# Attention backward in a fused block: query-major E by TensorE transposes and word copies instead of recomputed scores

## The chip, the cores and the metric

The kernel runs on 1 core of one Trainium2 chip. Time is device microseconds of one execution; three runs of the kernel before took 2842.46, 2846.36 and 2848.7 us, so the median is 2846.36 us.

## The reference

The program is forward and backward of a block `out = x + A(xn) * silu(B(xn))` with `xn = layernorm(x)`: A is multi-head attention, B is a layernorm and an MLP. It returns `out` and the gradients of seven inputs. S = 2048 tokens, D = 512, H = 32 heads of 16 numbers each, F = 1792, all in bf16. What concerns the change is attention and its backward:

```python
qkv = (x @ wqkv).reshape(B, S, 3, H, Dh).transpose(2, 0, 3, 1, 4)
q, k, v = qkv[0], qkv[1], qkv[2]
scores = jnp.einsum("bhqd,bhkd->bhqk", q, k) * (Dh ** -0.5)
p = _softmax(scores, axis=-1)
o = jnp.einsum("bhqk,bhkd->bhqd", p, v)
return o.transpose(0, 2, 1, 3).reshape(B, S, D) @ wo
...
_out, _vjp = jax.vjp(_f, A_x, A_wqkv, A_wo, B_w1, B_b1, B_w2, B_b2)
```

With E = exp(scores - bound) and G = E * (dO v^T), the outputs o and dq are sums over keys of E and G, and dk and dv are sums over queries of E and G. The first kind of sum wants E and G with keys on the partitions, the second with queries on the partitions.

## The kernel before

There are three phases: layernorms, projections and the MLP's forward (`phase_pre`), attention forward and backward together (`attention_core`), and the rest of the backward (`phase3`). The change lies in `attention_core` alone, whose instructions stand in the order in which its Python emits them, engine by engine (`tc.manual_schedule()`).

The 32 heads go as 16 pairs. A pair has 4 query chunks of 512 queries; a pair with a query chunk is a block (64 blocks), and a block has 16 steps, one for each key block `kb` of 128 keys. The two heads of a pair are `hj` 0 and 1. `KVT` and `QDT` hold a pair's operands with 32 rows for each of k (or q) of both heads and v (or dO) of both heads, so a matmul over them uses a quarter of the array's rows; the sums X and Z use a quarter of the columns each.

Step g does, for its key block:
- **s**, L649: scores, keys on partitions, both heads into one tile of two PSUM banks; ScalarE makes `et` from them (L677, 1024 wide). It is emitted one step ahead.
- **d**, L663: dO v^T, a bank for each head (`ps_d`, two banks); VectorE multiplies it with `et` into `gts` (L698, 512 wide, twice a step).
- **l, e, g**, L730, L733 and L745, of the step before: sums over keys into X (row sums of E, E with v and k, G with k). After 16 steps X is copied to `xs` (L751, VectorE).
- a query block of the block before, by `b_unit`: the sums over queries. They need E and G with queries on the partitions. For G, SyncE issues DMA transposes `gk<-gts` (L711), one every two steps. For E there are two ways: query blocks 1 and 3 of each key chunk come by DMA transposes `ek<-et` (L717; `dma_units`), the other two are computed again: **t**, L635, scores with queries on the partitions into the same two-bank pool as s (`ps_st`, two tiles), and a second exponential `e` (L685, 1024 wide). Then `Z<-e` or `Z<-ek` (L808) and `Z<-gk` (L814) add to Z, 64 partitions for one key chunk of 512 keys. After the four query blocks VectorE adds Z to `acc` (L819, L821).

```python
        emit_t(g)
        if not first:
            emit_le(g - 1)
        emit_exp_b(g)
        emit_s(g + 1)
        emit_d(g)
        emit_mult(g)
        emit_exp_a(g + 1)
        emit_dmat(g)
        if first:
            emit_le(g - 1)
        emit_g(g - 1)
        emit_z(g - lagb, 0)
        emit_z(g - lagb, 1)
```

One step after a block's last, `emit_finalize` transposes `xs` on TensorE (`XT`, L761, in one of d's banks), VectorE copies it (`xt`, L763) and computes three small tiles, and GpSimd makes the weights W1 and W2 that Z needs. The next pair's operands are loaded by `load_ops` in the second block of a pair: plain loads, copies into `KVPad` and `QDPad` on GpSimd, two DMA transposes `KVT` and `QDT` on SyncE (L595, L603).

Of the kernel before, what the change touches and what calls it, by code (L numbers as in the profile page):

```python
# [542 lines left out]
def attention_core(ctx, tc, NAT_s, NATQ_s, Oall, dQall, dKVT_out, ident_f32, npairs=16, nqc=4):  # L543
    nc = tc.nc
    dma_units = tuple((kc, qb) for kc in range(4) for qb in (1, 3))
    lagb = 3
    sb = lambda name, bufs: ctx.enter_context(tc.tile_pool(name=name, bufs=bufs))
    opnd = sb("opnd", 1)
    ps_st = ctx.enter_context(tc.tile_pool(name="ps_st", bufs=2, space=PSUM))
    ps_d = ctx.enter_context(tc.tile_pool(name="ps_d", bufs=2, space=PSUM))  # L550
# [3 lines left out]
    gtp = sb("gtp", 4)  # L554
    gbp = sb("gbp", 5)
    ekp = sb("ekp", 10)
    ep = sb("ep", lagb + 2)
    xsp = sb("xsp", 1)
    finp = sb("finp", 2)
# [12 lines left out]
    KVPad = opnd.tile([128, 16, 4, 32], bf16, name="KVPad")  # L572
    QDPad = opnd.tile([128, 16, 4, 32], bf16, name="QDPad")
    nc.gpsimd.memset(KVPad[:], 0.0)
    nc.gpsimd.memset(QDPad[:], 0.0)
# [4 lines left out]
    acc = opnd.tile([64, S], f32, name="acc")  # L580

    def load_ops(p):
        t = OP[p % 2]

        def plain():
            nc.sync.dma_start(out=t["NAT"][:].rearrange("q k j c -> q k (j c)"), in_=NAT_s[p])
            nc.sync.dma_start(out=t["NATQq"][:].rearrange("q k j c -> q k (j c)"), in_=NATQ_s[0][p])
            nc.sync.dma_start(out=t["NATQd"][:].rearrange("q k j c -> q k (j c)"), in_=NATQ_s[1][p])

        def ck():  # L590
            nc.gpsimd.tensor_copy(out=KVPad[:, :, 0:2, 0:17], in_=t["NAT"][:, :, :, 0:17])
            nc.gpsimd.tensor_copy(out=KVPad[:, :, 2:4, 0:16], in_=t["NAT"][:, :, :, 17:33])

        def tk():
            nc.sync.dma_start_transpose(out=t["KVT"][:].rearrange("r (m k) -> r m k", m=16),  # L595
                                        in_=KVPad[:].rearrange("q m j c -> q (m j c)"))

        def cq():
            nc.gpsimd.tensor_copy(out=QDPad[:, :, 0:2, 0:17], in_=t["NATQq"][:])
            nc.gpsimd.tensor_copy(out=QDPad[:, :, 2:4, 0:16], in_=t["NATQd"][:])  # L600

        def tq():
            nc.sync.dma_start_transpose(out=t["QDT"][:].rearrange("r (m k) -> r m k", m=16),  # L603
                                        in_=QDPad[:].rearrange("q m j c -> q (m j c)"))
        return [plain, ck, cq, tk, tq]
# [4 lines left out]
    st_s, st_t, st_d, st_et, st_e, st_gt = {}, {}, {}, {}, {}, {}  # L610
# [6 lines left out]
    def b_unit(g):  # L617
        j = g // 16 - 1
        return (j, (g % 16) // 4, g % 4) if 0 <= j < NB else None
# [4 lines left out]
    def emit_t(g):  # L624
        b = b_unit(g)
        if b is None or b[1:] in dma_units:
            return
        j, kc, qb = b
        op = op_of(j)
        q0 = (blocks[j][1] * 4 + qb) * 128  # L630
        t = ps_st.tile([128, 2, 512], f32, name="t", tag="st")
        st_t[g] = t
        for hj in range(2):
            r = 32 * hj
            nc.tensor.matmul(t[:, hj, :], lhsT=op["QDT"][r:r + 32, q0:q0 + 128], rhs=op["KVT"][r:r + 32, kc * 512:(kc + 1) * 512],  # L635
                             start=True, stop=True, tile_position=(r, 0))

    def emit_s(g):
        a = a_unit(g)
        if a is None:  # L640
            return
        j, kb = a
        op = op_of(j)
        qc = blocks[j][1]
        s = ps_st.tile([128, 2, 512], f32, name="s", tag="st")
        st_s[g] = s
        for hj in range(2):
            r = 32 * hj
            nc.tensor.matmul(s[:, hj, :], lhsT=op["KVT"][r:r + 32, kb * 128:(kb + 1) * 128], rhs=op["QDT"][r:r + 32, qc * 512:(qc + 1) * 512],  # L649
                             start=True, stop=True, tile_position=(r, 0))  # L650

    def emit_d(g):
# [6 lines left out]
        ds = []  # L659
        for hj in range(2):  # L660
            r = 64 + 32 * hj
            d = ps_d.tile([128, 512], f32, name="d", tag="d")
            nc.tensor.matmul(d[:], lhsT=op["KVT"][r:r + 32, kb * 128:(kb + 1) * 128], rhs=op["QDT"][r:r + 32, qc * 512:(qc + 1) * 512],  # L663
                             start=True, stop=True, tile_position=(r, 0))
            ds.append(d)
        st_d[g] = ds

    def emit_exp_a(g):
        a = a_unit(g)
        if a is None:  # L670
            return
        kb = a[1]
        if kb % 4 == 0:
            cur["et"] = etp.tile([128, 4, 4, 2, 128], bf16, name="et")
        et = cur["et"]
        st_et[g] = et
        nc.scalar.activation(out=et[:, :, kb % 4, :, :].rearrange("k b h q -> k h b q"),  # L677
                             in_=st_s.pop(g)[:].rearrange("k h (b q) -> k h b q", b=4), func=ACT.Exp)

    def emit_exp_b(g):  # L680
        if g not in st_t:
            return
        e = ep.tile([128, 2, 512], bf16, name="e")
        st_e[g] = e
        nc.scalar.activation(out=e[:], in_=st_t.pop(g)[:], func=ACT.Exp)  # L685

    def emit_mult(g):
# [8 lines left out]
        ds = st_d.pop(g)  # L696
        for hj in range(2):
            nc.vector.tensor_tensor(out=gts[:, kb % 2, hj, :].rearrange("k (b q) -> k b q", b=4), in0=ds[hj][:].rearrange("k (b q) -> k b q", b=4),  # L698
                                    in1=st_et[g][:, :, kb % 4, hj, :], op=ALU.mult)

    def emit_dmat(g):
# [10 lines left out]
        if kb % 4 == 3:  # L712
            for qb in range(4):
                if (kc, qb) in dma_units:
                    ek = ekp.tile([128, 8, 128], bf16, name="ek")
                    blk[j]["Ek"][(kc, qb)] = ek
                    nc.sync.dma_start_transpose(out=ek[:], in_=st_et[g][:, qb].rearrange("k a h q -> k (a h q)"))  # L717

    def emit_le(g):
# [4 lines left out]
        if kb == 0:  # L724
# [4 lines left out]
        for hj in range(2):  # L729
            nc.tensor.matmul(X[64 + 32 * hj:96 + 32 * hj, :], lhsT=Lc[:], rhs=et[:, :, kb % 4, hj, :],  # L730
                             start=(kb == 0), stop=False, skip_group_check=True, tile_position=(0, 64 + 32 * hj))
        for hj in range(2):
            nc.tensor.matmul(X[32 * hj:32 * hj + 32, :], lhsT=NATt[:, kb, hj, 1:33], rhs=et[:, :, kb % 4, hj, :],  # L733
                             start=(kb == 0), stop=(kb == 15), tile_position=(0, 32 * hj))

    def emit_g(g):
        a = a_unit(g)
        if a is None:
            return
        j, kb = a  # L740
        X = blk[j]["X"]
        NATt = op_of(j)["NAT"]
        gts = st_gt[g]
        for hj in range(2):
            nc.tensor.matmul(X[64 + 32 * hj:64 + 32 * hj + 17, :], lhsT=NATt[:, kb, hj, 0:17], rhs=gts[:, kb % 2, hj, :],  # L745
                             start=False, stop=(kb == 15), skip_group_check=True, tile_position=(0, 64 + 32 * hj))
        st_et.pop(g)
        st_gt.pop(g)
        if kb == 15:
            xs = xsp.tile([128, 512], f32, name="xs")  # L750
            nc.vector.tensor_copy(out=xs[:], in_=X[:])  # L751
            blk[j]["xs"] = xs

    def emit_finalize(j):
        p, qc = blocks[j]
        NQq = op_of(j)["NATQq"]
        NQd = op_of(j)["NATQd"]
        xs = blk[j].pop("xs")
        XT = ps_d.tile([128, 4, 128], f32, name="XT", tag="d")
        for qb in range(4):  # L760
            nc.tensor.transpose(XT[:, qb, :], xs[:, qb * 128:(qb + 1) * 128], ident_f32[:])  # L761
        xt = finp.tile([128, 4, 128], f32, name="xt")
# [14 lines left out]
        nc.vector.scalar_tensor_tensor(out=ndr[:], in0=dl[:], scalar=-1.0, in1=rL[:], op0=ALU.mult, op1=ALU.mult)  # L777
        nc.gpsimd.tensor_tensor(out=W1[:, :, :, 0:16], in0=ndo, in1=bc(rL[:]), op=ALU.mult)  # L778
        nc.gpsimd.tensor_tensor(out=W2[:, :, :, 16:32], in0=nqs, in1=bc(rL[:]), op=ALU.mult)
# [13 lines left out]
    def emit_z(g, part):  # L793
        b = b_unit(g)
        if b is None:
            return
        j, kc, qb = b
        p, qc = blocks[j]
        if part == 0:
            if qb == 0:  # L800
                cur["Z"] = ps_z.tile([64, 512], f32, name="Z", tag="z")
            Z = cur["Z"]
            if (kc, qb) in dma_units:
                ev = blk[j]["Ek"].pop((kc, qb))[:].rearrange("q (a h) k -> q h a k", h=2)
            else:
                ev = st_e.pop(g)[:].rearrange("q h (a k) -> q h a k", a=4)
            for hj in range(2):
                nc.tensor.matmul(Z[32 * hj:32 * hj + 32, :], lhsT=blk[j]["W1"][:, qb, hj, :], rhs=ev[:, hj],  # L808
                                 start=(qb == 0), stop=False, tile_position=(0, 32 * hj))
            return  # L810
        Z = cur["Z"]
# [155 lines left out]
```

## Time and profile before

| | us |
|---|---|
| median of three runs | 2846.36 |
| profiled execution, span | 2837.7 |
| PE busy | 2383.5 (84%) |
| VectorE (DVE) busy | 2013.4 (71%) |
| ScalarE (ACT) busy | 1739.4 (61%) |
| GpSimd (POOL) busy | 620.1 (22%) |
| `gts` multiplies L698, 2048 of them | 681 ns each |
| `et` exponentials L677, 1024 of them | 1024 ns each |
| `e` exponentials L685, 512 of them | 1023 ns each |
| DMA, mean | 192 GB/s, under 512 B 1,754,785 of 1,831,694 packets |

The profiled execution's own time is its span of 2837.7 us, from its first to its last instruction; the runs' times lie some 9 us above it. Busy times are of the whole program and overlap; the duration of a matmul holds its way through the array, so the distance between starts tells more than the duration. `x2` in a timeline row stands for two instructions of one kind in a row, and brackets hold the idle time before it and what ended it.

### The profile page before, as it was taken

The page shows a single profiled execution, that of the slowest core. Times are in us where ns is not written, and L with a number is a line of the kernel's source. Part 1 is how long each engine was busy: PE and PEld are TensorE (multiplying, and loading weights), DVE is VectorE, ACT ScalarE, POOL GpSimd, SP SyncE. Part 2 cuts the span into 40 slices and gives each one's busy share as a digit, 9 for nine tenths or more (in the row PEclk, how much of TensorE's full clock was granted, in tenths as well). Part 3 has the DMA queues.
Part 4 walks back from the last instruction along what each step waited for, and adds up shares of the span by engine and source line. Part 5 has one row for each costly group of instructions (what it writes and reads, how often), then busy time and mean ns, then how long its engine had stood idle before and what let it go on. Part 6 is the DMA issues. An engine that isn't in the chain of part 4 may idle for free. (4 is left out here: it accounts for less than half of the span.)

```text
span 2837.7 us, 49038 instructions
## 1 busy us (share of the span) xinstructions
PE 2383.5 (84%) x18885; PEld 779.8 (27%) x18944; DVE 2013.4 (71%) x3382; ACT 1739.4 (61%) x1973; POOL 620.1 (22%) x1023
## 2 busy tenths in 40 slices
PE   3786998989989998998989999899999857665967
PEld 2332222222222222222222222222222333332443
DVE  5764887878778787887878778788778638880044
ACT  3442777777777777777777777777777535440020
POOL 0434111101011110111101111110111328870024
PEclk8898899999999999999999999999999978887989
DMA  5434999999999999999999999999999853326331
GB/s 178 110 131 121 213 224 225 219 221 226 220 225 225 221 218 222 229 218 227 220 224 219 231 219 221 224 224 226 217 225 225 214 168 98 103 82 162 110 131 41
DMA packets 1831694, 543.46 MB, mean 192 GB/s; under 512 B 1754785, under 2 KB 1815586, under 8 KB 1831458
## 3 DMA queue, kind: packets, MB, share of 16 engines
q1 hardware_dynamic: 1758066, 486.70, 84.1%
q10 hardware_dynamic: 73392, 53.62, 6.1%
q8 instruction: 148, 2.42, 0.4%
q14 instruction: 88, 0.72, 0.1%
HBM read 65.41 MB, written 55.32 MB: 43 GB/s over the span
## 5 line engine op out<-in xcount | busy, mean ns | idle before, releaser
L698 DVE TENSOR_TENSOR gts<-d,et 128x512 bf16<-128x512 f32 x2048 | 1301.5, 681 | 379.4 <-issue 229.6
L677 ACT ACTIVATE et<-s 128x1024 bf16<-128x1024 f32 x1024 | 1000.5, 1024 | 29.8 <-PE d L663 11.5
L685 ACT ACTIVATE e<-t 128x1024 bf16<-128x1024 f32 x512 | 523.7, 1023 | 457.3 <-PE t L635 453.9
L663 PE MATMUL d<-QDT,KVT 32*128 32x512 bf16 x2048 | 598.1, 383 | 150.2 <-DVE gts L698 148.5
L649 PE MATMUL s<-QDT,KVT 32*128 32x512 bf16 x2048 | 402.8, 390 | 18.2 <-DMA QDT<-QDPad 13.2
L730 PE MATMUL X<-et,Lc 128*32 128x512 bf16 x2048 | 404.3, 391 | 14.3 <-DVE xs L751 14.3
L733 PE MATMUL X<-et,NAT 128*32 128x512 bf16 x2048 | 404.7, 392 | 0.0
L745 PE MATMUL X<-gts,NAT 128*17 128x512 bf16 x2048 | 402.4, 389 | 0.0
L814 PE MATMUL Z<-gk,W 128*32 128x512 bf16 x2048 | 401.0, 385 | 0.0
L778 POOL TENSOR_TENSOR W<-NATQd,rL 128x128 bf16<-128x128 bf16 x64 | 25.7, 402 | 1365.7 <-DVE rL L773 1365.7
L745 PEld LDWEIGHTS <-NAT 128*17 128x17 bf16 x2048 | 92.5, 87 | 491.5 <-issue 491.5
L808 PE MATMUL Z<-e,W 128*32 128x512 bf16 x1024 | 202.5, 389 | 4.7 <-DVE acc L821 2.3
L808 PE MATMUL Z<-ek,W 128*32 128x512 bf16 x1024 | 204.4, 395 | 0.0
L635 PE MATMUL t<-KVT,QDT 32*128 32x512 bf16 x1024 | 201.5, 390 | 0.0
L649 PEld LDWEIGHTS <-KVT 32*128 32x128 bf16 x2048 | 97.5, 91 | 361.7 <-issue 361.5
L663 PEld LDWEIGHTS <-KVT 32*128 32x128 bf16 x2048 | 138.7, 91 | 108.7 <-issue 80.4
L730 PEld LDWEIGHTS <-Lc 128*32 128x32 bf16 x2048 | 103.9, 93 | 181.6 <-issue 181.6
L821 DVE TENSOR_TENSOR acc<-Z,acc 64x512 f32<-64x512 f32 x192 | 129.1, 672 | 13.7 <-PE Z L814 13.7
L808 PEld LDWEIGHTS <-W 128*32 128x32 bf16 x2048 | 121.2, 93 | 57.4 <-issue 51.6
L733 PEld LDWEIGHTS <-NAT 128*32 128x32 bf16 x2048 | 101.3, 96 | 52.7 <-issue 3.5
L814 PEld LDWEIGHTS <-W 128*32 128x32 bf16 x2048 | 104.1, 96 | 8.2 <-issue 0.6
L635 PEld LDWEIGHTS <-QDT 32*128 32x128 bf16 x1024 | 48.3, 91 | 205.1 <-issue 205.1
(200 smaller groups left out, 2583.7 us busy)
## 6 DMA issues: line engine op xcount, KB each, us to landing
gk<-gts SPq DMA_TRANSPOSE x512, 4.1
ek<-et SPq DMA_TRANSPOSE x512, 3.1
HG_s<-hg SPq DMA_DIRECT2D x16, 448.0 KB, 3.1
DH_s<-dh ACTq DMA_DIRECT2D x16, 448.0 KB, 2.5
NAT<-NAT_s SPq DMA_DIRECT2D x16, 264.0 KB, 3.1
GB_s<-gB ACTq DMA_DIRECT2D x16, 256.0 KB, 2.0
dKVT_s<-ob SPq DMA_DIRECT2D x16, 256.0 KB, 3.4
dhc<-DH_s ACTq DMA_DIRECT2D x2, 2048.0 KB, 13.9
```

What stands on the lines that cost most here:

```text
L635: nc.tensor.matmul(t[:, hj, :], lhsT=op["QDT"][r:r + 32, q0:q0 + 128], rhs=op["KVT"][r:r + 32, kc * 512:(kc + 1) * 512], start=True, stop= ...
L649: nc.tensor.matmul(s[:, hj, :], lhsT=op["KVT"][r:r + 32, kb * 128:(kb + 1) * 128], rhs=op["QDT"][r:r + 32, qc * 512:(qc + 1) * 512], start ...
L663: nc.tensor.matmul(d[:], lhsT=op["KVT"][r:r + 32, kb * 128:(kb + 1) * 128], rhs=op["QDT"][r:r + 32, qc * 512:(qc + 1) * 512], start=True, ...
L677: nc.scalar.activation(out=et[:, :, kb % 4, :, :].rearrange("k b h q -> k h b q"), in_=st_s.pop(g)[:].rearrange("k h (b q) -> k h b q", b= ...
L685: nc.scalar.activation(out=e[:], in_=st_t.pop(g)[:], func=ACT.Exp)
L698: nc.vector.tensor_tensor(out=gts[:, kb % 2, hj, :].rearrange("k (b q) -> k b q", b=4), in0=ds[hj][:].rearrange("k (b q) -> k b q", b=4), ...
L730: nc.tensor.matmul(X[64 + 32 * hj:96 + 32 * hj, :], lhsT=Lc[:], rhs=et[:, :, kb % 4, hj, :], start=(kb == 0), stop=False, skip_group_check ...
L733: nc.tensor.matmul(X[32 * hj:32 * hj + 32, :], lhsT=NATt[:, kb, hj, 1:33], rhs=et[:, :, kb % 4, hj, :], start=(kb == 0), stop=(kb == 15), ...
L745: nc.tensor.matmul(X[64 + 32 * hj:64 + 32 * hj + 17, :], lhsT=NATt[:, kb, hj, 0:17], rhs=gts[:, kb % 2, hj, :], start=False, stop=(kb == 1 ...
L808: nc.tensor.matmul(Z[32 * hj:32 * hj + 32, :], lhsT=blk[j]["W1"][:, qb, hj, :], rhs=ev[:, hj], start=(qb == 0), stop=False, tile_position= ...
L814: nc.tensor.matmul(Z[32 * hj:32 * hj + 32, :], lhsT=blk[j]["W2"][:, qb, hj, :], rhs=gv[:, :, :, hj, qb, :], start=False, stop=(qb == 3), t ...
L821: nc.vector.tensor_tensor(out=av, in0=Z[0:64, :], in1=av, op=ALU.add)
```

## The change

The recomputed scores t and their exponential `e` are gone. E with queries on the partitions now comes from `et` alone: query block 3 of each key chunk by DMA transpose (a quarter), query blocks 0 to 2 by eight 128x128 transposes on TensorE into one PSUM bank (`tT`, new L694), which ScalarE copies to `ek` as 512 words of 32 bits, two bf16 numbers in each. A batch is emitted in three of four steps, four steps or more behind the exponential that made its `et`.

PSUM is dealt out anew: s has a bank for each head (`ps_st`, three tiles of one bank, shared with `tT`), and so ScalarE runs two 512-wide exponentials instead of one of 1024; `ps_d` has three banks instead of two. Two key chunks lie side by side in Z on 128 partitions, `acc` is `[128, 2, 512]`, and successive steps go to the lower and the upper half in turn (`ZORD`), so `acc` is added to twice a block instead of four times. `xs` moves from VectorE to ScalarE, `emit_finalize` is split in two and comes a step later, Z comes two steps later. `KVPad` and `QDPad` become one tile `Pad`, so the loads' order is copy, transpose, copy, transpose; a pair's result is stored with two DMAs instead of one. Buffers: `gtp` 4 to 3, `gbp` 5 to 7, `ekp` 10 to 19, `finp` 2 to 1, `ep` gone.

```diff
-    dma_units = tuple((kc, qb) for kc in range(4) for qb in (1, 3))
-    lagb = 3
-    ps_st = ctx.enter_context(tc.tile_pool(name="ps_st", bufs=2, space=PSUM))
-    ps_d = ctx.enter_context(tc.tile_pool(name="ps_d", bufs=2, space=PSUM))
+    ps_st = ctx.enter_context(tc.tile_pool(name="ps_st", bufs=3, space=PSUM))
+    ps_d = ctx.enter_context(tc.tile_pool(name="ps_d", bufs=3, space=PSUM))
...
-    gtp = sb("gtp", 4)
-    gbp = sb("gbp", 5)
-    ekp = sb("ekp", 10)
-    ep = sb("ep", lagb + 2)
+    gtp = sb("gtp", 3)
+    gbp = sb("gbp", 7)
+    ekp = sb("ekp", 19)
...
-    acc = opnd.tile([64, S], f32, name="acc")
+    acc = opnd.tile([128, 2, 512], f32, name="acc")
...
-        return [plain, ck, cq, tk, tq]
+        return [plain, ck, tk, cq, tq]
...
+    ZORD = [((i // 8) * 2 + i % 2, (i % 8) // 2) for i in range(16)]
...
+    def emit_s(g, hj):
...
+        s = ps_st.tile([128, 512], f32, name="s", tag="st")
+        nc.tensor.matmul(s[:], lhsT=op["KVT"][r:r + 32, kb * 128:(kb + 1) * 128], rhs=op["QDT"][r:r + 32, qc * 512:(qc + 1) * 512],
+                         start=True, stop=True, tile_position=(r, 0))
...
+        nc.scalar.activation(out=et[:, :, kb % 4, hj, :], in_=s[:].rearrange("k (b q) -> k b q", b=4), func=ACT.Exp)
...
         if kb % 4 == 3:
-            for qb in range(4):
-                if (kc, qb) in dma_units:
-                    ek = ekp.tile([128, 8, 128], bf16, name="ek")
-                    blk[j]["Ek"][(kc, qb)] = ek
-                    nc.sync.dma_start_transpose(out=ek[:], in_=st_et[g][:, qb].rearrange("k a h q -> k (a h q)"))
+            ek = ekp.tile([128, 8, 128], bf16, name="ek")
+            blk[j]["Ek"][(kc, 3)] = ek
+            nc.sync.dma_start_transpose(out=ek[:], in_=st_et[g][:, 3].rearrange("k a h q -> k (a h q)"))
+
+    def t_unit(g):
+        a = a_unit(g - 4)
+        if a is None or a[1] % 4 == 3:
+            return None
+        return a[0], a[1] // 4, a[1] % 4
+
+    def emit_T(g):
...
+        et = st_et[j * 16 + kc * 4 + 3]
+        t = ps_st.tile([128, 8, 128], bf16, name="tT", tag="st")
+        for b in range(8):
+            nc.tensor.transpose(t[:, b, :], et[:, qb, b // 2, b % 2, :], ident_bf[:])
+        st_T[g] = t
+
+    def emit_cT(g):
...
+        ek = ekp.tile([128, 8, 128], bf16, name="ek")
+        blk[j]["Ek"][(kc, qb)] = ek
+        nc.scalar.copy(out=ek[:].rearrange("q a k -> q (a k)").bitcast(f32),
+                       in_=st_T.pop(g)[:].rearrange("q a k -> q (a k)").bitcast(f32))
...
+            for hj in range(2):
+                r = 64 * par + 32 * hj
+                nc.tensor.matmul(Z[r:r + 32, :], lhsT=blk[j]["W2"][:, qb, hj, :], rhs=gv[:, :, :, hj, qb, :],
+                                 start=(qb == 0), stop=False, skip_group_check=True, tile_position=(0, r))
...
+    FIN_AT = 2
+    ZG, ZE = -5, -5
...
+        emit_z(g + ZG - 16, 1)
+        emit_z(g + ZE - 16, 0)
+        emit_acc(g + ZE - 16)
+        emit_s(g + 1, 0)
+        emit_XT(g)
+        emit_d(g, 0)
+        emit_d(g, 1)
+        emit_s(g + 1, 1)
+        emit_mult(g)
+        emit_fin(g)
+        emit_T(g)
+        emit_x(g - 1, "l")
+        emit_x(g - 1, "e")
+        emit_x(g - 1, "g")
+        emit_xs(g - 1)
+        emit_cT(g)
+        emit_dmat(g)
```

## The prediction

> **What bounds the kernel now.** I read the page's slices first, then the table of stretches for a quiet part of the attention, then the timeline of some of its steps, then the waits, and last the DMA issues of SyncE.
>
> ```profile
> PE   3786998989989998998989999899999857665967
> DVE  5764887878778787887878778788778638880044
> ACT  3442777777777777777777777777777535440020
> ...
> DMA  5434999999999999999999999999999853326331
> ```
> ```profile
> 800.00:1200.00 400.00, 363.49 (x3195) 98.12 (x3196) 315.77 (x537) 299.67 (x314) 57.88 (x150) 0.99 1.14 222
> ```
> The second fence is one row of the table of stretches: busy time of PE, PEld, DVE, ACT and POOL, then granted clock, DMA share and GB/s. Attention fills slices 5 to 31 and no engine but PE comes near full: in 400 us PE is busy 363, DVE 316, ACT 300. The first multiply `gts` starts at 283.47 us, the last step's at 2222.42; 1,023 steps between them make 1.895 us a step, 30.3 us for a block of 16 steps, 1,940 us for the 64 blocks. Everything else (some 900 us) the change doesn't touch. So the question is what one step costs.
>
> ```profile
> 999.95 0.39 PE L635 MATMUL t<-KVT,QDT 32*128 32x512 bf16 x2
> 1000.27 0.39 PE L730 MATMUL X<-et,Lc 128*32 128x512 bf16 x2
> 1000.28 0.39 PE L733 MATMUL X<-et,NAT 128*32 128x512 bf16 x2
> 1000.60 0.39 PE L649 MATMUL s<-QDT,KVT 32*128 32x512 bf16 x2
> 1000.61 0.39 PE L663 MATMUL d<-QDT,KVT 32*128 32x512 bf16 x2
> 1000.93 0.39 PE L745 MATMUL X<-gts,NAT 128*17 128x512 bf16 x2
> 1000.93 0.39 PE L808 MATMUL Z<-ek,W 128*32 128x512 bf16 x2
> 1001.16 0.38 PE L814 MATMUL Z<-gk,W 128*32 128x512 bf16 x2
> ...
> 1002.47 0.37 PE L663 MATMUL d<-QDT,KVT 32*128 32x512 bf16 x1 [0.23 <-DVE gts L698]
> ...
> 1003.31 0.39 PE L635 MATMUL t<-KVT,QDT 32*128 32x512 bf16 x2
> ```
> Starts count here, not durations. Matmuls on different quarters of the array start together: l (L730) and e (L733), s and d, g (L745) and `Z<-ek`. A pass that keeps its way of cutting the array (columns after columns) frees its quarters after 0.22 us (1000.93 to 1001.16); one followed by another cut, rows after columns or the reverse, after 0.32 (999.95 to 1000.27, 1000.28 to 1000.60). From the same timeline the passes of these two steps, without waits, are .32+.33+.32+.22 for t, le, sd, g with Z, then .22 and .31 for Z with the next l and for e, then .32+.22+.31: 2.57 us. They take 3.36 (999.95 to 1003.31), and the next two, with an `acc` on DVE, 3.65: 7.0 for four steps. The rest is waiting, and the row at 1002.47 says for what: d has two banks, and its next one is free only when `gts` has multiplied the one before. The waits put numbers to this and to a second limit:
>
> ```profile
> PE d L663 <- DVE gts L698: 148.5, 525, 3.7
> ...
> DVE gts L698 <- DMA gk<-gts: 58.3, 30, 4.5
> ```
> ```profile
> 1001.29 4.44 SPq L711 DMA_TRANSPOSE gk<-gts  x2
> 1005.83 2.65 SPq L717 DMA_TRANSPOSE ek<-et  x2
> 1008.58 3.58 SPq L711 DMA_TRANSPOSE gk<-gts  x2
> ```
> SyncE issues transposes without a pause, 7.29 us for the four of four steps. Matched in order, a `gk` transpose lands 9.0 us (median; 5.3 to 13.6 at the 5th and 95th percentile) after the multiply that fills its source has ended. When the loads of the next pair come between, it falls behind and `gts` finds no free buffer. Most blocks take 29.5 us from one `XT` to the next; these stalls make the mean 30.3.
>
> **The change part by part, for four steps (PE first).** Gone are t and ScalarE's exponential of it (two in four steps) and one of two `ek` transposes by DMA. Added are three batches T of eight 128x128 transposes. Their price comes from phase 3:
>
> ```profile
> 2426.13 0.61 PE L384 MATMUL h_tp<-ident_bf,h1T 128*128 128x128 bf16 x8
> ```
> ```profile
> 2433.46 1.54 ACT L422 COPY dh1T<-dh_tp 128x512 bf16<-128x512 bf16 x3
> ```
> Eight transposes span 0.61 with 0.22 for one alone, so they follow at 0.056; a batch and the cut after it take 7 x 0.056 + 0.15 = 0.54 (0.15: from the last f32 transpose `XT` to the next pass 0.205 passes where two of them are 0.109 apart, so 0.10 for the cut). From rows to the whole array the trace of before shows nothing; columns to the whole array took 0.31 (`Z` to `XT`) and 0.37 (`Z` to L52 at 2226.4), and I take 0.32, as for the other cuts.
>
> The Trainium skill, "TensorE: Matmul & The Clock Gate", section Back-to-back issue gap, speaks against this change: in a stream of weight loads and matmuls 128 columns wide it gives about 81 ns each; an estimate by it adds 8 x 0.025 us to each batch, 2.4 us to a block, which would turn the forecast below into 2,900 us, slower than before.
>
> The rest of the step on PE: s, d stay one pass (.32). l and e stay one pass, now followed by g without a new cut (.22). `Z<-gk` comes straight after g: in steps where Z is in the lower half of the partitions the two run together, as g and `Z<-ek` do at 1000.93, in the others it waits .22. `Z<-ek` follows on the same columns (.22) and a cut (.32) leads back to s. A step with T and the upper half is .32+.54+.22+.22+.22+.32 = 1.84; with the lower half 1.62; the step without T (every fourth, always lower half) .32+.22+0+.22+.32 = 1.08. Four steps: 1.84+1.62+1.84+1.08 = 6.38, against 5.14 before. So PE gets more to do; what may shrink is the waiting, 7.0 less 5.14.
>
> Does it? d now has three banks. d starts, DVE starts .51 later (1000.61 to 1001.12), multiplies follow at .60; the first d's bank is back .51+.69+.05 = 1.25 us after it and wanted one step later, the second's 1.85 and two steps: no wait. DVE has 8 x .60, half an `acc` of 128x512 (.30; two of 64 rows before, .60) and no `xs`: 5.1 in four steps, plus 1.35 a block for `xt` and the three small ones. ScalarE: two 1024-wide exponentials start .92 apart, three 512-wide copies take 1.54, so .48 each; 8 halves and 3 word copies are 5.3, as much as before (6 x .91 = 5.5), and `xs` adds .48 a block. The 32-bit copy reads and writes f32: L260, f32 to f32 of that size, has a mean of 595 ns, L422 585, so no other price; were it twice that, ScalarE would have 6.7 and be the bound. Single banks for s and T make one wait: T's bank is the one its copy of the step before empties; two exponentials and a copy after s put that at .51+.96+.59+.05 = 2.11 after s, and PE is back at T after 1.94 in the step whose Z overlaps: .17, once in four. So 6.55 for four steps, 26.2 for sixteen.
>
> Once a block comes the finalization, 1.5 us before (29.5 less 4 x 7.0). After: `XT` stands between s and d and adds a cut and its own 4 x .109 and a cut, .85; it holds one of d's banks until `xt`, which is behind two multiplies, at .85+.51+1.20+.69+.05 = 3.30 after s, while d of the next step wants it at 2.47: .83; `xs` on ScalarE puts the T copy back by .48. Together 2.2. A block: 28.4.
>
> SyncE loses one `ek` in four (1.3 of 7.29), so 6.0 for 6.55: it no longer falls behind all the time. Its queue also passes one store more per pair, and `Pad`, now one tile, spreads the two operand transposes over eight steps: both lie in that slack. Against it, `gts` has three buffers instead of four: a transpose must land four steps (6.6 us) after its source is full, not six (11.4). Issue and landing alone are 1.8 + 2.2, so it fits if the queue isn't behind. Of the .8 us a block that stalls cost now I keep .4; the bounds are 0 and the second rival. W is ready 4.8 us after s of that step (`xt` done at 3.28, two small DVE steps, POOL's three of .40) and Z wants it at 5.7: nothing. `gbp` and `ekp` hold as many tiles as Z's longer lag keeps alive (7 and 18 or 19), and the word copy that takes the last one needs a Z a whole copy earlier: nothing. Moving Z two steps later costs two steps at the very end, and a tail without t and its exponentials gives that back: nothing.
>
> The sum: 28.8 us a block, 1,843 us instead of 1,940: 97 less. The profiled execution spans 2837.7 us, the median of the runs is 2846.4, 8.7 above it; the same 97 from the median give 2,750 (2,741 for the span).
>
> **The rivals.** (1) Slower: the transposes don't keep 0.056 between row and column passes. The place is T, 96 transposes a block, and the gain of 1.5 us a block is gone at 0.072 each. The row for it: L421 and L52 show many intervals of 0.107, twice the usual (in stages where the page's clock row stands at 7 or 8). At 0.107 throughout a block is 28.8 + 96 x .051 = 33.7, the kernel 3,063. Against: in attention the granted clock is 0.99, and PE gets busier. A tenth more for each of the two cuts around T would do the same (24 x .1 = 2.4 a block, 2,903). I give 0.16 to the two, the milder end more.
> (2) Slower: the DMA queue. If landing stayed at its 9.0 us, four steps could not be shorter than that: 2.25 a step, 2,304 us, 3,210 in all; it costs more than the change gains from 7.6 us up (four of the present steps). For: 84 in 100 landings are later than 6.6 now. Against: that lag is a queue with 7.29 of 7.4 us filled. 0.07.
> (3) A larger gain: waits of T's bank and of `XT` vanish under the spare time of DVE and ScalarE, stalls too: 4 x 6.38 + 1.5 = 27.0 a block, 2,634. 0.12.
> (4) No difference: passes and waits trade evenly, block 30.2 to 30.4; 0.05.
>
> **How the numbers follow.** Forecast 0.60 (2,680 to 2,830, its bounds being stalls of 0 or .8, waits of T and `XT` from half to full, and a cut of .35 for .32). Within 0.2%, about 6 us, a measurement of this kernel can't tell a difference. Faster 0.60 + 0.12 = 0.72; same 0.05; slower 0.23. The range 2,630 to 2,890 takes in the forecast, (3), (4) and the mild end of (1), and leaves out about 0.2.
>
> **What would show it.** Right: the wait of d for `gts` (148.5 us) falls below 60; T batches of 0.61 spans; PE idle below a tenth, ACT and DVE at 0.75 to 0.85; blocks of 28 to 29 us between `XT`s; `gk` landing 4 to 6 us after its multiply. Wrong: T pace above 0.07, cuts above 0.4, `gts` waiting for DMA by more than 60 us, or ScalarE without idle time.

## The result, and the profile after

The changed kernel took 2738.36 us (median of four runs, 2735.35 to 2740.01), the kernel before beside it 2847.23 us. The ratio is 0.9621, its 95% interval 0.9607 to 0.9634: about 109 us faster, where 97 were forecast. The profiled execution spans 2738.2 us, 99.5 less than that of before.

The slices of the page, after:

```profile
PE   3687799999999999999999999999999666656967
...
DVE  5755677787777787777778778777778458870144
...
DMA  5334999999999999999999999999999643326331
```

The same stretch of 400 us as before, in the table of stretches (busy time of PE, PEld, DVE, ACT and POOL, then granted clock, DMA share and GB/s):

```profile
800.00:1200.00 400.00, 383.36 (x4494) 169.06 (x4491) 313.67 (x528) 331.39 (x625) 53.27 (x144) 1.00 1.05 199
```

PE's row of the slices now stands at 9 throughout attention, and in the quiet stretch PE is busy 383 us of 400 where it was 363. ScalarE rose from 300 to 331, VectorE is where it was, DMA moves 199 GB/s instead of 222. A high busy share does not by itself mean little waiting: a matmul counts as busy for some 0.38 us although the next may start 0.22 us after it, so short waits hide in it. The kernel with two d banks, shown below, has PE busy 393 of 400 us and is 95 us slower than this one. The same 400 us hold more steps now. From the first `gts` multiply to the last step's a step takes 1.795 us (1.895 before), a block 28.7 (30.3): over 64 blocks 103 us.

What a step is made of shows in PE's timeline:

```profile
1016.53 0.39 PE L629 MATMUL s<-QDT,KVT 32*128 32x512 bf16 x1
...
1016.86 0.62 PE L694 MATMUL tT<-ident_bf,et 128*128 128x128 bf16 x8
1017.41 0.39 PE L719 MATMUL X<-et,Lc 128*32 128x512 bf16 x2
...
1017.63 0.38 PE L725 MATMUL X<-gts,NAT 128*17 128x512 bf16 x2
1017.64 0.38 PE L800 MATMUL Z<-gk,W 128*32 128x512 bf16 x2
1017.86 0.38 PE L807 MATMUL Z<-ek,W 128*32 128x512 bf16 x2
1018.17 0.38 PE L629 MATMUL s<-QDT,KVT 32*128 32x512 bf16 x1
...
1019.33 0.39 PE L725 MATMUL X<-gts,NAT 128*17 128x512 bf16 x2
1019.54 0.39 PE L800 MATMUL Z<-gk,W 128*32 128x512 bf16 x2
```

From s to T 0.33, T and the cut after it 0.55, l with e 0.22, then g, and `Z<-gk` 0.01 behind it where Z is in the lower half (1017.63, 1017.64) and 0.21 behind it where Z is in the upper half (1019.33, 1019.54). The step from 1016.53 to 1018.17 has no wait in it at all. Four steps, from the s at 1015.23 to the one at 1021.72, take 6.49 us; 7.0 before. (In the program's order a T stands two steps or more behind the last exponential of its `et`, not four; no T is seen to wait for an exponential.)

The waits, and two rows that show where one of them sits:

```profile
PE tT L694 <- ACT ek L704: 39.7, 62, 0.8
...
PE d L647 <- DVE gts L660: 30.8, 73, 1.5
...
DVE gts L660 <- DMA gk<-gts: 14.3, 13, 2.6
```
```profile
1003.71 0.61 PE L694 MATMUL tT<-ident_bf,et 128*128 128x128 bf16 x8 [0.64 <-ACT ek L704]
...
1005.53 0.66 PE L744 MATMUL XT<-ident_f,xs 128*128 128x128 f32 x4
```

d's wait for its bank went from 148.5 us in 525 places to 30.8 in 73, the wait of `gts` for a free buffer from 58.3 to 14.3. This view counts only time in which PE was idle, so it shows the smaller part. Added up from one PE start to the next, the distances among s and d take 7.49 us of a block in the kernel before and 1.39 now (over the same 56 blocks as in the table below). That is 6.1 us a block less waiting. PE's passes without waits rose by 4.8, from 4 x 5.14 = 20.6 to 25.4. New is T's wait for its bank, 39.7 us in 62 places, once a block: in the step where `xs` stands ahead of the copy on ScalarE (1003.71). A `gk` transpose lands 4.9 us (median; 3.8 to 7.9 at the 5th and 95th percentile) after its source is full, where it took 9.0. SyncE no longer issues without a pause: a `gk` transpose begins to issue 0.2 us (median) after its source is full, where it began 4.5 us after.

### The profile page after: what moved, and what is told of

The parts are those of the page before. It is cut to its first block, busy times and chain, and to the rows that moved or that the text cites. A ratio compares the mean times of both kernels' runs of the same rounds, so it can differ in the third digit from the quotient of the medians.

```text
span 2738.2 us, 61100 instructions
## 1 busy us (share of the span) xinstructions
PE 2372.0 (87%) x24005; PEld 1079.3 (39%) x24064; DVE 1910.5 (70%) x3190; ACT 1795.8 (66%) x3317; POOL 600.6 (22%) x990
## 5 line engine op out<-in xcount | busy, mean ns | idle before, releaser
L635 ACT ACTIVATE et<-s 128x512 bf16<-128x512 f32 x2048 | 1127.3, 597 | 305.8 <-PE s L629 211.7
L694 PE MATMUL tT<-ident_bf,et 128*128 128x128 bf16 x6144 | 475.1, 220 | 40.1 <-ACT ek L704 39.7
L629 PE MATMUL s<-QDT,KVT 32*128 32x512 bf16 x2048 | 478.2, 386 | 16.8 <-DMA QDT<-Pad 15.2
L647 PE MATMUL d<-QDT,KVT 32*128 32x512 bf16 x2048 | 443.1, 384 | 31.0 <-DVE gts L660 30.8
L704 ACT COPY ek<-tT 128x512 f32<-128x512 f32 x768 | 456.7, 595 | 0.8 <-PE tT L694 0.8
L694 PEld LDWEIGHTS <-et 128*128 128x128 bf16 x6144 | 353.8, 98 | 213.5 <-issue 199.2
L807 PE MATMUL Z<-ek,W 128*32 128x512 bf16 x2048 | 390.4, 379 | 0.0
L771 POOL TENSOR_TENSOR W<-NATQq,rL 128x128 bf16<-128x128 bf16 x64 | 25.5, 399 | 1223.6 <-DVE rL L766 1223.6
L421 PE MATMUL dh_tp<-ident_bf,dh 128*128 128x128 bf16 x224 | 30.1, 270 | 76.7 <-DVE dh L418 73.9
L448 PE MATMUL ps_dw<-dm_all,hgc 128*128 128x512 bf16 x220 | 54.8, 406 | 29.7 <-DMA hgc<-HG_s 29.4
```

The lines of the kernel that those rows point to most:

```text
L448: nc.tensor.matmul(ps[:], lhsT=hgc[:, t, :], rhs=dm_all[:, t, :], start=(t == 0), stop=(t == NT - 1))
L629: nc.tensor.matmul(s[:], lhsT=op["KVT"][r:r + 32, kb * 128:(kb + 1) * 128], rhs=op["QDT"][r:r + 32, qc * 512:(qc + 1) * 512], start=True, ...
L635: nc.scalar.activation(out=et[:, :, kb % 4, hj, :], in_=s[:].rearrange("k (b q) -> k b q", b=4), func=ACT.Exp)
L694: nc.tensor.transpose(t[:, b, :], et[:, qb, b // 2, b % 2, :], ident_bf[:])
L704: nc.scalar.copy(out=ek[:].rearrange("q a k -> q (a k)").bitcast(f32), in_=st_T.pop(g)[:].rearrange("q a k -> q (a k)").bitcast(f32))
L807: nc.tensor.matmul(Z[r:r + 32, :], lhsT=blk[j]["W1"][:, qb, hj, :], rhs=ev[:, hj], start=False, stop=(qb == 3), skip_group_check=True, til ...
```

## The experiments

Twelve kernels were run. One is the kernel before with one edit, the others are the changed kernel with one or more; times are medians, "more" and "less" are against its 2738.36 us, and the ratio is to the kernel before on the same chip. (The kernel before took 2846.6 to 2847.3 us beside each group of runs, so times of different groups can be compared.) To see where each edit goes, the table adds up the distances from one PE start to the next over 56 blocks of each trace and divides by 56 (us per block). "Into T" is from s to the first transpose, "in T" between transposes, "around d" the distances among s and the two d (some 0.2 of it without any wait), "g to Z" from g to `Z<-gk`, "XT" all of the finalization's transposes with their cuts; the rest is every other distance.

| kernel | us | ratio, 95% | into T | in T | around d | g to Z | XT | rest | block |
|---|---|---|---|---|---|---|---|---|---|
| changed | 2738.4 | 0.9607–0.9634 | 4.57 | 4.80 | 1.39 | 1.87 | 0.90 | 15.27 | 28.80 |
| 12 transposes | 2861.4 | 1.0038–1.0075 | 4.52 | 7.48 | 0.85 | 1.73 | 0.90 | 15.21 | 30.70 |
| two d banks | 2833.0 | 0.9942–0.9970 | 3.81 | 4.82 | 3.71 | 1.73 | 0.90 | 15.21 | 30.18 |
| 16-bit copy | 2834.4 | 0.9948–0.9973 | 6.42 | 4.71 | 1.15 | 1.82 | 0.90 | 15.23 | 30.24 |
| E all by T | 2836.8 | 0.9948–0.9973 | 6.12 | 6.34 | 0.56 | 1.82 | 0.90 | 14.56 | 30.31 |
| E half by DMA | 2896.9 | 1.0159–1.0204 | 3.41 | 3.33 | 5.25 | 1.76 | 0.90 | 16.60 | 31.26 |
| two `gts` buffers | 2958.7 | 1.0365–1.0419 | 4.44 | 4.87 | 4.47 | 1.83 | 0.92 | 15.53 | 32.06 |
| XT later | 2696.3 | 0.9451–0.9479 | 4.24 | 4.78 | 1.10 | 1.87 | 0.81 | 15.26 | 28.05 |
| Z in turn | 2713.8 | 0.9517–0.9553 | 4.39 | 4.77 | 2.49 | 0.39 | 0.90 | 15.28 | 28.23 |
| both | 2681.8 | 0.9397–0.9431 | 4.10 | 4.80 | 2.31 | 0.39 | 0.81 | 15.38 | 27.78 |
| XT later, four `gts` | 2672.1 | 0.9365–0.9396 | 4.26 | 4.78 | 0.75 | 1.88 | 0.81 | 15.23 | 27.71 |
| both, four `gts` | 2633.7 | 0.9231–0.9267 | 4.07 | 4.76 | 1.68 | 0.39 | 0.81 | 15.25 | 26.95 |

### What the transposes on PE cost

A batch of twelve transposes, four of them done twice:

```diff
-        for b in range(8):
+        for b in [0, 1, 2, 3, 0, 1, 2, 3, 4, 5, 6, 7]:
```

> The changed kernel with twelve transposes in each T batch instead of eight (four are done twice). Theory (PE's passes set the step now): 12 batches x 4 x 0.0555 us = 2.7 us more a block, 170 us in all, about 2,908 us. Rival (ScalarE, VectorE or the DMA queue sets the step and PE has slack): less than 40 us more, under 2,780 us.

2861.36 us, 123 more, where the theory had 170, and 0.4 to 0.8% slower than the kernel before. PE's timeline of this kernel:

```profile
1015.71 0.84 PE L694 MATMUL tT<-ident_bf,et 128*128 128x128 bf16 x12
1016.48 0.39 PE L719 MATMUL X<-et,Lc 128*32 128x512 bf16 x2
```

From T to l 0.77 instead of 0.55, so the four take 0.055 each; the 48 of a block are the 2.68 us that the table shows (4.80 to 7.48). But the block grew by 1.9 only: the waits around d gave back 0.54, since a longer step leaves more time for d's bank. PE's passes do set most of the step: some seven tenths of what is added to them is paid.

### The third bank of d

d gets back two banks; the fourth goes to the pool of s and T, where `XT` moves:

```diff
-    ps_st = ctx.enter_context(tc.tile_pool(name="ps_st", bufs=3, space=PSUM))
-    ps_d = ctx.enter_context(tc.tile_pool(name="ps_d", bufs=3, space=PSUM))
+    ps_st = ctx.enter_context(tc.tile_pool(name="ps_st", bufs=4, space=PSUM))
+    ps_d = ctx.enter_context(tc.tile_pool(name="ps_d", bufs=2, space=PSUM))
...
-        XT = ps_d.tile([128, 4, 128], f32, name="XT", tag="d")
+        XT = ps_st.tile([128, 4, 128], f32, name="XT", tag="st")
```

> The changed kernel with two d banks, as before, and four for s, T and XT. Theory (the third d bank is what took the waits away): the second d waits for a multiply that ends 1.85 us after the last one, while steps are 1.84, 1.62, 1.84 and 1.08 long, so 1.0 us in four steps; less up to 1.4 us a block for T's and XT's bank, 2.6 to 4 us a block, 2,900 to 2,990 us. Rival (the gain came from the relief of the DMA queue, d's banks do little): under 2,760 us.

2833.01 us, 95 more: the direction was right, the size expected was too high. Two rows of PE's timeline:

```profile
1019.77 0.37 PE L647 MATMUL d<-QDT,KVT 32*128 32x512 bf16 x1 [0.33 <-DVE gts L660]
1020.37 0.37 PE L647 MATMUL d<-QDT,KVT 32*128 32x512 bf16 x1 [0.23 <-DVE gts L660]
```

Both d of a step wait for a multiply again. Around d a block spends 2.3 us more (the view of waits shows only 38.4 us of it in all, 30.8 before the edit: the rest hides in PE's busy time); the bank given to s and T removes T's wait in the step of `xs` (into T 4.57 to 3.81), so 1.4 is left. The two PSUM decisions are one budget: the third bank is worth 2.3 us a block to d and would be worth 0.8 to T.

### The word copy on ScalarE

```diff
-        nc.scalar.copy(out=ek[:].rearrange("q a k -> q (a k)").bitcast(f32),
-                       in_=st_T.pop(g)[:].rearrange("q a k -> q (a k)").bitcast(f32))
+        nc.scalar.copy(out=ek[:], in_=st_T.pop(g)[:])
```

> The changed kernel with the word copy of T as 1024 bf16 numbers instead of 512 words. Theory (PE bounds, ScalarE has 5.4 us of work in four steps of 6.5): ScalarE comes to 8 x 0.485 + 3 x 0.91 + 0.12 = 6.7 us and passes PE by a little, and T's bank comes back 0.43 us later: 1 to 2 us a block, 2,800 to 2,870 us. Rival (ScalarE has slack enough to hide it): within 10 us of 2,738 us.

2834.40 us, 96 more, within what was expected. A copy of 1024 bf16 numbers takes 1,021 ns (median) where 512 words take 595. The stretch from 800 to 1200 us and the wait of T:

```profile
800.00:1200.00 400.00, 367.06 (x4285) 166.65 (x4284) 298.90 (x501) 376.18 (x596) 53.19 (x140) 1.00 0.98 192
```
```profile
PE tT L694 <- ACT ek L704: 126.3, 258, 1.3
```

ScalarE is now busiest, 376 of 400 us, and PE waits for it at T in 258 places instead of 62. So the word copy is what keeps ScalarE off the path; without it the change gains 13 us.

### How E is split between PE and the DMA queue

All of E by T, no `ek` transpose left:

```diff
         if kb % 4 == 3:
-            ek = ekp.tile([128, 8, 128], bf16, name="ek")
-            blk[j]["Ek"][(kc, 3)] = ek
-            nc.sync.dma_start_transpose(out=ek[:], in_=st_et[g][:, 3].rearrange("k a h q -> k (a h q)"))
...
-        if a is None or a[1] % 4 == 3:
+        if a is None:
```

> The changed kernel with all of E by TensorE transposes and none by DMA: four T batches in four steps, SyncE issues gk alone. Theory (PE sets the step): four more batches a block with a cut each, 0.54 + 0.32 us, less the pass they stand beside, so 2.2 to 3.4 us a block, and less stalls 0.2: 2,865 to 2,945 us. Rival (the queue still holds the step back): below 2,780 us.

2836.84 us, 98 more; the size expected was too high. Four more batches a block add 3.1 us to the distances into T (1.55) and in T (1.54) and take 0.7 out of the rest. DMA falls to 159 GB/s in the quiet stretch, a `gk` transpose lands after 3.8 us, and `gts` waits for a buffer once in the whole run. The waits around d fall by 0.8. Again PE is the bound and part of what it gains in work comes out of waits.

Half of E by DMA, as in the kernel before, and two batches in four steps (and `ekp` 20):

```diff
-            ek = ekp.tile([128, 8, 128], bf16, name="ek")
-            blk[j]["Ek"][(kc, 3)] = ek
-            nc.sync.dma_start_transpose(out=ek[:], in_=st_et[g][:, 3].rearrange("k a h q -> k (a h q)"))
+            for qb in (2, 3):
+                ek = ekp.tile([128, 8, 128], bf16, name="ek")
+                blk[j]["Ek"][(kc, qb)] = ek
+                nc.sync.dma_start_transpose(out=ek[:], in_=st_et[g][:, qb].rearrange("k a h q -> k (a h q)"))
...
-        if a is None or a[1] % 4 == 3:
+        if a is None or a[1] % 4 >= 2:
```

> The changed kernel with half of E by DMA transpose, as before, and two T batches in four steps instead of three. Theory (the DMA queue was a bound of its own before and still is at that load): PE's passes fall by 0.86 us in four steps, but SyncE's four transposes take 7.3 us again, so a block is 29 to 31 us and the kernel 2,770 to 2,880 us. Rival (only PE's passes count, the queue hides): 28.5 less 3.4 = 25.1 us a block, about 2,520 us.

2896.94 us, 159 more and above what was expected: slower than the kernel before, though PE has least to do of all these kernels. The stretch and the wait that carries it:

```profile
800.00:1200.00 400.00, 350.76 (x3742) 141.07 (x3738) 285.55 (x483) 285.06 (x526) 47.98 (x128) 0.97 1.14 216
```
```profile
DVE gts L660 <- DMA gk<-gts: 220.7, 103, 6.0
```

No engine is full, not even PE at 351 of 400; DMA stands at 216 GB/s and `gts` waits 221 us for a buffer. A landing takes 7.5 us (median). The granted clock is 0.97 in this stretch, 1.00 in the changed kernel; what that adds to the 159 us wasn't separated. So with three `gts` buffers the quarter left to DMA is the best of the three shares tried: a quarter less costs 98 us, on PE, a quarter more 159 us, mostly in stalls. Half of E by DMA with four `gts` buffers, as many as the kernel before has, wasn't run; the last kernels below show that a fourth buffer takes away most stalls at nearly this load, so the best share with four is open.

Two buffers for `gts` instead of three, to see the second rival's mechanism by itself:

```diff
-    gtp = sb("gtp", 3)
+    gtp = sb("gtp", 2)
```

> The changed kernel with two gts buffers instead of three. Theory (the second rival's mechanism: a gk transpose must land before its buffer is wanted, now two steps after its source is full): landing took 3.8 us at the least and 4.9 in the median in the changed kernel, so two steps cannot be shorter than about 4.0 to 4.9 us, 32 to 39 us a block, 2,950 to 3,400 us. Rival (landing is hidden whatever the number of buffers): under 2,780 us.

2958.69 us, 220 more, at the low end of what was expected.

```profile
DVE gts L660 <- DMA gk<-gts: 294.2, 223, 3.8
...
PE d L647 <- DVE gts L660: 173.9, 198, 3.6
```

With two buffers a transpose must land two steps (3.6 us at the pace of the changed kernel) after its source is full; it takes 4.3 (median). The multiply waits, d's banks wait behind it, and PE behind those. The mechanism of the rival exists; three buffers are just clear of it.

The other side of the same question, the kernel before with only query block 3 by DMA and three recomputed:

```diff
-    dma_units = tuple((kc, qb) for kc in range(4) for qb in (1, 3))
+    dma_units = tuple((kc, qb) for kc in range(4) for qb in (3,))
```

> The kernel before with a quarter of E by DMA transpose instead of half; the scores of the other three query blocks are computed again. Theory (two limits in the kernel before: the waits of d, which stay, and the queue, which is relieved): the stalls of 0.8 us a block go, one t pass of 0.32 us and one exponential of 0.91 come in four steps, partly under the waits of d: 29.5 to 30.5 us a block, 2,795 to 2,860 us. Rival (the queue set the pace of the kernel before, and its relief alone is the gain): under 2,750 us.

2839.75 us, within what was expected; ratio 0.998 (0.9969 to 0.9992) to the kernel before. The queue's stalls are gone (`gk` lands after 4.7 us), and d's wait, which was expected to stay, fell too:

```profile
PE s L649 <- ACT et L677: 107.5, 437, 2.0
...
PE d L663 <- DVE gts L698: 56.9, 251, 0.2
```

But the fourth recomputed exponential puts ScalarE at 345 of 400 us, and s waits for its tile 107.5 us in all. The relief of the DMA queue, bought that way, is worth 0.2%: what it gives is nearly all paid for the score pass and the exponential. What it would be worth at no price isn't shown. T with the word copy makes it cheaper.

### What the new order still costs

The change puts `XT` between s and d. Here it stands after the second s, just ahead of T, on the same cut of the array:

```diff
-        emit_XT(g)
         emit_d(g, 0)
         emit_d(g, 1)
         emit_s(g + 1, 1)
+        emit_XT(g)
```

> The changed kernel with XT moved from between s and d to just before the T batch, so that it shares T's cuts and takes its bank of d after the two d of its step. Theory (finalization costs PE 0.85 us of passes and 0.8 us of waiting for d's bank in each block): 1.2 us less a block, about 2,660 us. Rival (that time is under VectorE's chain of xt and the small steps anyway): within 15 us of 2,738 us.

2696.27 us, 42 less; more was expected.

```profile
1015.95 0.38 PE L629 MATMUL s<-QDT,KVT 32*128 32x512 bf16 x1
1016.27 0.66 PE L744 MATMUL XT<-ident_f,xs 128*128 128x128 f32 x4
1016.76 0.61 PE L694 MATMUL tT<-ident_bf,et 128*128 128x128 bf16 x8
```

`XT` and T now share one cut: 0.43 us a block (into T 4.57 to 4.24, XT 0.90 to 0.81). Around d another 0.29. T's own wait stays. What was expected beyond that is partly eaten by the next limit: with shorter blocks `gts` waits 34.1 us for its buffers, 14.3 before the edit. The changed kernel thus pays 42 us for where it puts `XT`.

Z's key chunks one after the other, all in the lower half, `acc` as `[64, S]` and added four times a block, a pair's result stored with one DMA, as in the kernel before (and `gbp` six):

```diff
-    acc = opnd.tile([128, 2, 512], f32, name="acc")
+    acc = opnd.tile([64, S], f32, name="acc")
...
-    ZORD = [((i // 8) * 2 + i % 2, (i % 8) // 2) for i in range(16)]
+    ZORD = [(i // 4, i % 4) for i in range(16)]
...
-        par = kc % 2
+        par = 0
```

> The changed kernel with every key chunk of Z in the lower half of the columns, one after the other, as before; acc in 64 rows, four additions a block instead of two. Theory (PE's passes set the step, and Z in the upper half cannot run beside g): 8 x 0.22 = 1.8 us less a block on PE, at most 0.6 of it given back by waits for acc: 27.0 to 27.6 us a block, 2,625 to 2,665 us. Rival (VectorE's two more additions or the DMA queue take over at once): 2,720 us or more.

2713.79 us, 25 less; three times that was the least expected, and the rival's 2,720 is nearer. Most of the pass is gained: g to Z falls by 1.48 us a block, from 1.87 to 0.39 (1.8 were expected), as g and `Z<-gk` now run together in nearly every step. But around d 1.10 comes back:

```profile
PE d L647 <- DVE gts L660: 56.4, 81, 2.7
...
DVE gts L660 <- DMA gk<-gts: 40.9, 23, 3.8
```

VectorE has twice as many `acc` additions (332 of 400 us busy, 314 before the edit) and a shorter step to do them in, and the `gts` buffers stall again; what the smaller `gbp` adds to that wasn't separated. So "two key chunks side by side" saves VectorE time and costs PE passes; here it costs more than it saves, by 25 us. Both edits together:

> Both together: Z in the lower half and XT next to T. Theory (passes and bank waits add up on PE): 2.4 to 3.0 us less a block than the changed kernel, 2,545 to 2,590 us. Rival (the DMA queue with 5.9 us in four steps, or VectorE with 5.8, is the next bound): not below 2,620 us.

2681.84 us, 57 less: the rival's case, the next bound. `gts` waits 60.0 us for DMA and the block of 27.8 has 2.31 around d. That names the next step, a fourth `gts` buffer (`gbp` is six as in the two kernels before it):

```diff
-    gtp = sb("gtp", 3)
-    gbp = sb("gbp", 7)
+    gtp = sb("gtp", 4)
+    gbp = sb("gbp", 6)
```

> Z in the lower half, XT next to T, and four gts buffers. Theory (of the 27.7 us of a block in the run without the fourth buffer 0.8 are stalls on gk, which a window of six steps takes up): 25 to 50 us below that run's 2,682, so 2,632 to 2,657 us. Rival (the queue is full at this pace, a buffer only moves the wait): within 12 us of 2,682 us.

2633.66 us, 48 less than without the fourth buffer and 105 less than the changed kernel, ratio 0.9249 to the kernel before and within what was expected.

```profile
800.00:1200.00 400.00, 387.95 (x4810) 173.37 (x4805) 348.63 (x595) 353.40 (x668) 63.29 (x164) 1.00 1.15 214
```
```profile
DVE gts L660 <- DMA gk<-gts: 4.2, 6, 1.2
```

DMA is as full as in the kernel with half of E by DMA (214 and 216 GB/s) and lands late (median 5.9 us, 10.1 at the 95th percentile), but with four buffers `gts` hardly waits for it. To see what the buffer does without the edit of Z, `XT` later with four `gts` buffers (and `ekp` 18):

> XT next to T and four gts buffers, with 18 ek tiles instead of 19 to make room; Z side by side as in the change. Theory: the blocks with stalls (0.3 us a block in the mean) come to 27.7 us, 2,675 to 2,690 us against 2,696 with three buffers. Rival (18 tiles make the word copy wait for Z, or the fourth buffer does nothing): 2,694 us or more.

2672.13 us, 24 less than `XT` later alone, slightly better than expected. Around d falls from 1.10 to 0.75. With the buffer, undoing the order of Z is worth 38 us (2672.13 to 2633.66); without it, also with `XT` later, 14 (2696.27 to 2681.84).

## Why the prediction was right, and where not

**The mechanism was right: more work on PE, fewer waits.** Passes were forecast to rise from 5.14 to 6.38 us in four steps; the table's 56 blocks have 25.4 a block, 6.34 in four. The waits around d, 7.3 us of a block before, are 1.2. A block was forecast at 28.8 us; these blocks have 28.80, the whole attention 28.7. One other thing moved: the granted clock over attention was 0.983 before and 0.997 after. An estimate: on all of before's passes, 20.6 us a block, that would be 0.3 us of the 1.6 gained; whether it is a cause or comes from the waits that are gone isn't shown. The signs that were named came: d's wait 30.8 (below 60), T batches of 0.61 to 0.62, PE idle 4% of the quiet stretch, VectorE at 0.78 and ScalarE at 0.83, blocks of 28.5 (median between `XT`s), landing 4.9.

**T and its cuts were right.** 0.056 between transposes, 0.149 from the last to l, 0.317 from rows to the whole array (medians), forecast 0.056, 0.15 and 0.32. The kernel with twelve transposes confirms the pace under a heavier load. The first rival is refuted: the pace is far from 0.072 and the cut from 0.40. The Trainium skill, "TensorE: Matmul & The Clock Gate", section Back-to-back issue gap, gives 81 ns in a sustained stream 128 columns wide; here 6,144 transposes in groups of eight follow at 56 ns (median), so the measurement decides against it, and its formula for an isolated gap (2.5 ns + 128/2.4 = 56 ns) is the one that agrees.

**Four steps: the sum was right, two terms were not.** Forecast 6.55 = 6.38 + 0.17 for T's bank. Measured: the block of 28.80 less what the finalization and the stalls take (0.90 for `XT`, 0.77 into T beyond 12 x 0.317, 1.2 around d beyond 0.2) is 25.9, or 6.48 for four. Outside the step of `xs` T waits for under 0.1 us a block; the term of 0.17 in four steps is not there. In its place stand 0.1 for pairs that start together: small distances of some 3 to 5 ns each, many in a step, which the forecast counted as nothing. That the sum still fits so closely is in part luck.

**The finalization and the stalls were sized too low, slightly.** Forecast 2.2 + 0.4 a block: 0.85 for `XT` (0.90 measured), 0.48 for `xs` ahead of T's copy (0.77), and together 1.23 for d's bank and the stalls (1.2). The kernel with `XT` later takes out 0.43 of `XT` and its cuts and 0.29 of the last. How the 1.2 divide between `XT`'s bank and the `gts` buffers isn't known exactly; with a fourth buffer and `XT` late 0.55 are left (0.75 less 0.2).

**The third bank and the word copy, each costed at "no wait" and "no other price", were right, and each carries nearly all of the gain.** Undone one at a time they cost 95 and 96 of the 109 us. So do a quarter of E moved to T (98) or to DMA (159). That is no contradiction: each undone part brings back one limit (d's bank, ScalarE, PE, the DMA queue) that by itself costs nearly the whole gain or more. The gain is not a sum over parts; it needs each of these. (For the share of E this holds with three `gts` buffers.) It does not need all of the change: two other parts, the place of `XT` and Z side by side, cost time.

**The DMA queue: right.** Landing was forecast at 4 to 6 us and is 4.9; three buffers suffice at that, barely: 14.3 us of stalls are left, two buffers or half of E by DMA make the rival true.

**What was not forecast** is that two parts of the change work against it. `XT` between s and d and Z on 128 partitions were costed about right on PE (0.85 a block, and 0.22 in half of the steps) but taken as given; undoing the first is worth 42 us, undoing the second, with the first undone and a fourth `gts` buffer, 38.

**The last 12 us** between 97 and 109: 9 of them are the step from the span to the median, which failed. The prediction subtracted 97 from the median; the spans of the two profiled executions differ by 99.5. The 8.7 us between before's span and its median were not work around the span: every later run of that kernel lies 1.7 to 1.9 us above its own span, as the changed kernel does (2740.01 and 2738.2). The profiled execution of before was a short one of a kernel whose runs spread from 2838 to 2854.

That the spans agree to 2.5 us is in part luck. The steps themselves gave 103 us. "Everything else", which the prediction left untouched, moved too: the tail from the last multiply to the last `acc` is 10 us shorter, the first multiply comes 4.9 us later, and the rest of the backward takes 602.0 us instead of 593.2. In all the kernels with the new order that rest takes 600.6 to 605.1 us, in the two with the old order 593.2 and 593.3. What makes it longer isn't shown.

## What to carry to other kernels

Sum the passes of the busiest engine by start-to-start distances, cuts included, and then ask of each shared resource (a PSUM bank, a buffer, a copy engine) whether it can keep that pace; here the gain appeared only when all of them did, so that undoing any one of three parts cost nearly all of it. When a stage becomes shorter, the time in which a buffer must come back shrinks with it: a buffer that cost nothing to save before the change may be the next bound after it. A layout that saves one engine's instructions should be priced on the engine that sets the pace: here side-by-side Z was cheaper for VectorE and dearer for PE.

## What the runs showed of the hardware

- Transposes of 128x128 bf16 in a row follow at 0.056 us between row-tiled and column-tiled passes, and the granted clock stays at 1.00 in that stretch, with three of four steps holding a batch; from rows to the whole array the next pass starts after 0.317, from columns to it after 0.310 (`Z` to `XT`, before). The Trainium skill, "TensorE: Matmul & The Clock Gate", Part 4: PE-mode transpose, says that the full clock does not engage for transposes; among other passes, as here, they did not lower it. A stretch of transposes alone is shown by no run here.
- Whether two passes of 32 columns run together depends on which columns they use: g with `Z<-gk` in the lower half some 5 ns apart, in the upper half 213 ns (medians).
- A ScalarE copy out of PSUM goes by the number of elements, not of bytes: 1,024 bf16 numbers take 1,021 ns, the same bytes as 512 words of 32 bits 595 ns.
- No kernel here moves more than 222 GB/s in the quiet stretch, and the landing time of a `gk` transpose (median) grows with the load: 3.8 us at 159 GB/s, 4.9 at 199, 5.9 at 214, 7.5 at 216, 9.0 at 222. What that costs depends on the buffers too: 4.2 us of stalls with four at 214 GB/s and 58.3 with four at 222, 220.7 with three at 216.
